# First three pairs: the causal mask added to the row-maximum blocks by TensorE instead of VectorE

## The chip, the cores and the metric

The kernel runs on one core of one Trainium2 chip. The metric is the device time of one execution in microseconds, the median of several runs.

## What is computed

The reference is a masked attention with a decay bias, whose output goes through a mixture of four attention experts, of which each row uses two. The part that the change touches is the subtraction of the row maximum under a causal mask:

```
scores = scale * q @ k.T                                   # 8 batches x 8 heads, 576 x 576, head_dim 64
bias   = -(cum[:, :, :, None] - cum[:, :, None, :])        # cum = running sum of max(s, 0)
scores = where(causal, -1e9, scores + minimum(bias, 0))
scores = scores - max(scores, axis=-1)
attn   = exp(scores); attn = attn / (sum(attn) + 1e-9); attn_out = attn @ v
# then per expert e: q, k, v = x @ wq[e], x @ wk[e], x @ wv[e]; the same masked softmax without bias;
# out += gate weight * (a @ v @ wo[e]) for the two best experts of each row
```

## The kernel before, in words

All work is cut into 50 steps called pairs: two heads of a batch (32 of them), two experts of a batch (16), or, twice near the end, projections alone. A pair's two heads are numbered j = 0 and 1. For each pair n the kernel splits q and k into a high and a low part (h and l steps, ScalarE, GpSimd and VectorE, L560 to L606), finds a maximum for every row, computes the transposed scores in PSUM chunks of 512 columns by two matmuls each (L687 and L692), takes the exponential on ScalarE (L708), clears the part above the diagonal on GpSimd (L726) and multiplies with v on TensorE (L844).

The row maxima come before the scores, because minus the maximum enters the scores as one more row of the second matmul (row 96 of Q2). They are found from bfloat16 products of q and k: the 576 rows are cut in nine blocks of 64, and block qt needs the columns 0 to 64 (qt + 1). The table MBANKS packs these blocks into six PSUM banks, called m0 to m5 as steps on TensorE and M0 to M5 as steps on VectorE; each entry has a slot, 0 to 8 for the blocks, and 9 for the left part of block 8, which is split in two.

- On TensorE (`bank`, L626) every slot is one matmul per head: 96 rows of contraction, 64 stationary columns, 64 to 512 moving columns. Head 0 writes PSUM partitions 0 to 63, head 1 partitions 64 to 127. LDWEIGHTS is an instruction of its own here.
- On VectorE (`reduce`, L640) every slot is one fused instruction that adds the mask (0, or -1e30 above the diagonal, in the last 64 columns of the block) and takes the maximum, followed by a second instruction that reads the accumulator into a column of `mcol`. The entry of slot 8 starts from the value of slot 9.
- When all nine columns are there, `mt` (TensorE, L660) transposes them, `mA` (ScalarE, L664) copies them with a minus sign, and `mq` (SyncE, L669) sends them by DMA into row 96 of Q2. The second matmul of every score chunk (L692) reads that row.

The order of all steps on all engines is one written list, STEPS; each engine executes its own instructions in that order, and PSUM banks are handed out in it (`take`, `give`), so that a bank given back by VectorE or ScalarE goes to a later step of TensorE. The maxima of pair n are computed during pairs n-2 and n-1. In the first 54 us the list also holds dummy matmuls (`idle`, L1325): 32 ahead of everything and 48 strewn between the steps (`z0` to `z47`); they write to a bank that nobody reads. The profile shows each as two records of 0.11 us.

`ident` (an identity in fp32) and `mask` (bfloat16) are made by GpSimd at the start.

Of the kernel before, what the change touches and what calls it, by code (L numbers as in the profile page):

```python
# [10 lines left out]
BF16 = mybir.dt.bfloat16  # L11
I32 = mybir.dt.int32
AF = mybir.ActivationFunctionType
OP = mybir.AluOpType
AX = mybir.AxisListType
# [3 lines left out]
S = 576  # L19
# [8 lines left out]

EARLY = 9
SUMMED = 4  # L30
FIRST_IDLE, IDLE = 32, 48
SCHUNKS = [
# [18 lines left out]
def chunks(n):  # L51
    return EARLY_SCHUNKS if n < EARLY else SCHUNKS
# [28 lines left out]
def heads(t, at, c0, c1):  # L81
# [5 lines left out]
MBANKS = [  # L87
# [6 lines left out]
]  # L94
# [239 lines left out]
def tile_attention_then_moe(ctx, tc, qk, vm, vt, s, wqk, wvg, wo, out):  # L334
    nc = tc.nc
# [25 lines left out]
    ident = PB[0][:, PSPARE : PSPARE + P]  # L361
# [5 lines left out]
    mask = const.tile([P, S], BF16, tag="mask", name="mask")  # L367
# [92 lines left out]
    def take(name):  # L460
        t = ps.tile([P, 512], F32, tag=f"bank{banks[0]}", name=name, bufs=1)
        taken[id(t)] = t, banks.pop(0)
        return t

    def give(t):
        banks.append(taken.pop(id(t))[1])
# [17 lines left out]
    mcol = {}  # L484
# [11 lines left out]
    def live(n):  # L496
        return 0 <= n < N and pairs[n][0] > 0
# [32 lines left out]
    def r2(n):  # L530
        return n % NQK2
# [82 lines left out]
    def maxima(n, banks):  # L614

        if not live(n):
            return {}
        items = {}

        def bank(bi):  # L620
            mbank[n, bi] = t = take(f"mx{n}_{bi}")
            for qt, k0, k1, c0, _ in MBANKS[bi]:
                for j in range(2):
                    q2 = Q2[r2(n)][:, j].bitcast(BF16)[:, 1::2]
                    k2 = K2[r2(n)][:, j].bitcast(BF16)[:, 1::2]
                    nc.tensor.matmul(  # L626
                        t[64 * j : 64 * j + 64, c0 : c0 + k1 - k0],
                        q2[0:RC, 64 * qt : 64 * qt + 64],
                        k2[0:RC, k0:k1],
                        start=True, stop=True,  # L630
                    )

        def reduce(bi):
            if n not in mcol:
                mcol[n] = sb.tile([P, 10], F32, tag="mcol", name=f"mcol{n}", bufs=2)
            t = mbank[n, bi]
            for qt, k0, k1, c0, slot in MBANKS[bi]:
                w = k1 - k0
                m0 = k0 + S - 64 * (qt + 1)
                nc.vector.tensor_tensor_reduce(  # L640
                    t[:, c0 : c0 + w], t[:, c0 : c0 + w], mask[:, m0 : m0 + w],
                    scale=1.0, scalar=mcol[n][:, 9:10] if slot == 8 else NEG, op0=OP.add, op1=OP.max,
                    accum_out=mcol[n][:, slot : slot + 1],
                )
            give(t)

        for bi in banks:
            items[f"m{bi}"] = lambda bi=bi: bank(bi)
            items[f"M{bi}"] = lambda bi=bi: reduce(bi)
        return items  # L650
# [24 lines left out]
    def scores(n):  # L675
# [49 lines left out]
        def lower(a, w):  # L725
            nc.gpsimd.affine_select(  # L726
                out=a, in_=a, pattern=[[0, a.shape[1]], [1, w]], compare_op=OP.is_ge,
                fill=0.0, base=0, channel_multiplier=-1,
            )

        def two_diags(ci):
            base = pchunk(n)[ci][0][0]
            lower(p[:, base : base + 1280].rearrange("p (b c) -> p b c", c=320)[:, :, 0:128], 128)

        def chunk_of(ci, c0, c1):
            at, o = pchunk(n)[ci]
            return heads(p, at, o + c0, o + c1)

        def sums_of():
            if n not in rtile:  # L740
                rtile[n] = sb.tile([P, 2, S], F32, tag="r", name=f"r{n}", bufs=3)
            return rtile[n]

        def first():
            r, a = sums_of()[:, :, 0:128], chunk_of(0, 0, 128)
            if n < SUMMED:
                nc.gpsimd.tensor_scalar(r, a, 1.0, 0.0, op0=OP.mult, op1=OP.add)
# [3 lines left out]
        def below(ci):  # L751
            if ci < 2 or n >= SUMMED:
                r = sums_of()
            if ci == 0 and n < EARLY:
                two_diags(0)
                add(r[:, :, 128:320], chunk_of(0, 128, 320), chunk_of(0, 320, 512), op=OP.add)
            elif ci == 0:
                lower(chunk_of(0, 224, 352), 128)
                nc.gpsimd.tensor_scalar(
                    r[:, :, 0:128], chunk_of(0, 224, 352), 1.0, 0.0, op0=OP.mult, op1=OP.add  # L760
                )
                lower(chunk_of(0, 0, 128), 128)
                add(r[:, :, 128:288], chunk_of(0, 352, 512), chunk_of(0, 0, 160), op=OP.add)
            elif ci == 1 and n < EARLY:
                add(r[:, :, 320:S], chunk_of(1, 0, 256), chunk_of(1, 256, 512), op=OP.add)
            elif ci == 1:
                add(r[:, :, 288:352], chunk_of(1, 0, 64), chunk_of(0, 160, 224), op=OP.add)  # L767
                add(r[:, :, 352:S], chunk_of(1, 64, 288), chunk_of(1, 288, 512), op=OP.add)
            elif ci == 2:
                two_diags(2)  # L770
                if n >= SUMMED:
                    for kt, q0, _, c in chunks(n)[2]:
                        add(r[:, :, q0:S], r[:, :, q0:S], chunk_of(2, c, c + S - q0), op=OP.add)  # L773
            else:
                a = heads(p, PTAIL, 0, 64)
                lower(a[0:64], 64)
                if n >= SUMMED:
                    nc.gpsimd.tensor_tensor(r[:, :, 512:S], r[:, :, 512:S], a, op=OP.add)
# [38 lines left out]
        if n < EARLY:  # L817
            items["e0"] = first
        if n < SUMMED:
            items["b0"] = early_sums  # L820
# [62 lines left out]
    def sums(n):  # L883

        if n not in quads or n < SUMMED:
            return {}
# [455 lines left out]
    def slot(n):  # L1342
# [11 lines left out]
        if n == N - 1:  # L1354
            steps.update(finish(n - 1, "x"))
            steps.update(finish(n, "y"))
            steps.update({{"v": "w", "V": "W"}[x[0]] + x[1:]: f for x, f in pv(n).items()})
            steps.update(numbered(proj_o(B - 2, range(4))))
            steps.update(out_here(B - 1))
        else:  # L1360
            steps.update(maxima(n + 1, (3, 4, 5)))
            steps.update(maxima(n + 2, (0, 1, 2)))
            steps.update(minus_max(n + 1))
            steps.update(hi(n + 2))
            steps.update(lo(n + 1))
            steps.update(sums(n - 1))
            steps.update(recip(n - 2))
            if n > -2:
                for x, f in enumerate(load(n + 3)):
                    steps["ld"] = f  # L1370
            for f in load_v(n):
                steps["lv"] = f
            for x, w in enumerate(WS.get(n, [])):
                steps[f"w{x}"] = w
# [62 lines left out]
```

## Time and profile before

| what | us |
|---|---|
| median of 3 runs (645.58, 645.64, 651.75) | 645.64 |
| the profiled execution | 645.95 |
| its span, first to last instruction | 644.2 |
| busy: TensorE matmul, weight load | 635.4 (99%), 543.0 (84%) |
| busy: VectorE, ScalarE, GpSimd | 546.1 (85%), 449.2 (70%), 433.3 (67%) |
| L640 fused maximum, 432 + 48 instructions; its accumulator reads | 194.2 (432 of them), 65.3 (480) |

The span is 1.7 us shorter than the execution, which also holds what lies before the first and behind the last instruction. A matmul's busy time covers its way through the array, and matmuls overlap: a 64-column one is shown with 0.19 to 0.22 us, while the next starts 0.06 us later. So the time that TensorE needs for one is read from the starts of neighbours, and a busy share of 99% leaves room for waits that are no longer than such an overlap.

### The profile page before, as it was taken

To read this page: it belongs to the slowest core of one execution; us is meant where nothing else is said; L and a number is where in the kernel's file an instruction comes from. 1 tells how busy PE (TensorE), PEld (TensorE's weight loads), DVE (VectorE), ACT (ScalarE), POOL (GpSimd) and SP (SyncE) were. 2 spreads that over 40 slices of the span, in tenths; PEclk is the share of its full clock that TensorE was granted. 3 is DMA by queue.
4 is the path that set the end of the run, shared out by engine and by line. 5 is a ranking of instruction groups with operands and counts; after the bars stand their busy time and mean duration, and the time that the engine had idled before them with its cause. 6 is when DMAs were issued, how large, how long until landed. Compare 5 with 4: busy or idle time off the path is not lost.

```text
span 644.2 us, 16548 instructions
## 1 busy us (share of the span) xinstructions
PE 635.4 (99%) x5990; PEld 543.0 (84%) x5990; DVE 546.1 (85%) x1440; ACT 449.2 (70%) x981; POOL 433.3 (67%) x530
## 2 busy tenths in 40 slices
PE   9999999999999999999999999999999999999997
PEld 9878898778878888888888898888987889789875
DVE  8988989898898978987898878898788978873984
ACT  6688767865877577766777766975685966566374
POOL 8786679686675868558766758559686777818030
PEclk9999999999999999999999999999999999999999
DMA  5356445436565375443756447475465634332323
GB/s 166 114 147 173 134 114 136 126 81 150 133 159 153 96 201 131 95 137 75 185 147 194 122 125 145 132 179 131 106 136 149 166 93 126 105 83 66 83 67 114
DMA packets 60879, 83.33 MB, mean 129 GB/s; under 512 B 26894, under 2 KB 35342, under 8 KB 60798
## 3 DMA queue, kind: packets, MB, share of 16 engines
q1 hardware_dynamic: 60798, 82.28, 49.0%
q8 instruction: 47, 0.77, 0.5%
q14 instruction: 34, 0.28, 0.2%
HBM read 44.55 MB, written 10.09 MB: 85 GB/s over the span
## 4 chain that ended last, share of the span: by engine, by line
PE 87%; DVE 6%; DMA 3%; issue 1%; ACT 1%; POOL 1%; SPq 0%; DVEq 0%; POOLq 0%
PE pvp L844 18%; PE pq L1078 16%; PE s L687 11%; PE s L692 10%; PE mx L626 9%; PE pw L1078 7%; PE po L1078 7%; PE sm L894 3%; DVE mx L640 3%; PE idle L1325 2%; DMA w_qk<-in_wqk_dram 2%; DMA rb<-rr 2%; PE po L1048 1%; PE mt L660 1%; PE gt L1205 1%
## 5 line engine op out<-in xcount | busy, mean ns | idle before, releaser
L640 DVE CUSTOM_DVE_ANT_0 mx<-mx,mask 128x256 f32<-128x256 f32 (+7 forms) x432 | 194.2, 468 | 33.2 <-PE mx L626 19.5
L708 ACT ACTIVATE p<-s 128x512 f32<-128x512 f32 x288 | 161.5, 588 | 60.9 <-PE s L692 57.7
L726 POOL TENSOR_SCALAR_AFFINE_SELECT p<-p 128x256 f32<-128x256 f32 (+2 forms) x183 | 112.7, 617 | 102.7 <-ACT p L708 96.1
L687 PE MATMUL s<-q,k 128*128 128x288 f32 (+5 forms) x672 | 168.9, 285 | 1.9 <-DVE mcol L640 0.8
L692 PE MATMUL s<-q,k 97*128 97x288 f32 (+5 forms) x672 | 160.9, 280 | 0.1
L687 PEld LDWEIGHTS s<-q,k 128*128 128x128 f32 (+1 forms) x672 | 122.5, 182 | 10.9 <-issue 4.7
L773 POOL TENSOR_TENSOR r<-r,p 128x640 f32<-128x640 f32 x84 | 120.8, 1438 | 6.8
L692 PEld LDWEIGHTS s<-q,k 97*128 97x128 f32 (+1 forms) x672 | 121.7, 182 | 1.3 <-DMA q<-mr 0.3
L600 DVE TENSOR_TENSOR q<-raw,q 64x576 fp32r<-64x576 f32 (+1 forms) x86 | 84.8, 995 | 19.1 <-ACT q L560 14.2
L844 PE MATMUL pvp<-p,v 128*64 128x320 f32 (+6 forms) x1024 | 96.3, 334 | 0.3 <-DVE mcol L640 0.3
L844 PEld LDWEIGHTS pvp<-p,v 128*64 128x64 f32 x1024 | 67.4, 137 | 25.5 <-issue 0.9
L605 DVE TENSOR_TENSOR k<-raw,k 64x576 fp32r<-64x576 f32 (+1 forms) x86 | 84.2, 986 | 5.5 <-DMA k<-k 3.5
L626 PE MATMUL mx<-k,q 96*64 96x256 bf16 (+7 forms) x960 | 81.2, 293 | 0.1
L1078 PE MATMUL pq<-xh,wqkh 128*128 128x288 f32 x256 | 76.3, 298 | 0.0
L1078 PE MATMUL pq<-xl,wqkh 128*128 128x288 f32 x256 | 75.5, 295 | 0.6 <-DVE xl L969 0.6
L1078 PE MATMUL pq<-xh,wqkl 128*128 128x288 f32 x256 | 75.4, 295 | 0.0
L626 PEld LDWEIGHTS <-q 96*64 96x64 bf16 x960 | 48.7, 109 | 20.7 <-issue 7.0
L563 ACT ACTIVATE k<-raw 64x576 fp32r<-64x576 f32 x96 | 64.6, 680 | 2.3 <-DMA raw<-in_qk_dram 0.6
L640 DVE DVE_READ_ACCUMULATOR2_ANT mcol<- 128x1 f32 x480 | 65.3, 136 | 0.9
L560 ACT ACTIVATE q<-raw 64x576 fp32r<-64x576 f32 x96 | 64.1, 679 | 1.9 <-DVE mcol L640 0.4
L858 ACT ACTIVATE pv<-pvp 128x320 f32<-128x320 f32 (+1 forms) x92 | 35.8, 402 | 33.1 <-PE pvp L844 32.8
L767 POOL TENSOR_TENSOR r<-p 128x128 f32<-128x128 f32 x37 | 21.5, 581 | 49.6 <-ACT p L708 49.5
(155 smaller groups left out, 1219.5 us busy)
## 6 DMA issues: line engine op xcount, KB each, us to landing
raw<-in_qk_dram SPq DMA_DIRECT2D x30, 576.0 KB
rb<-rr SPq DMA_DIRECT2D x92, 144.0 KB
q<-q SPq DMA_DIRECT2D x45, 288.0 KB
k<-k SPq DMA_DIRECT2D x39, 288.0 KB
v<-in_vm_dram SPq DMA_DIRECT2D x32, 256.0 KB
out_dram<-o SPq DMA_DIRECT2D x31, 256.0 KB
q<-mr SPq DMA_DIRECT2D x96, 2.2 KB
out_dram<-o SPq DMA_DIRECT2D x10, 128.0 KB
```

Source lines behind the costliest of these rows:

```text
L563: nc.scalar.activation(k2[0:64, j], get_raw(n, j)[64:128], AF.Copy)
L600: eng.tensor_tensor(a[64:128, j], get_raw(n, j)[0:64], q2[0:64, j].bitcast(F32), op=OP.subtract)
L605: eng.tensor_tensor(c[0:64, j], get_raw(n, j)[64:128], c[64:128, j].bitcast(F32), op=OP.subtract)
L626: nc.tensor.matmul(t[64 * j : 64 * j + 64, c0 : c0 + k1 - k0], q2[0:RC, 64 * qt : 64 * qt + 64], k2[0:RC, k0:k1], start=True, stop=True,)
L640: nc.vector.tensor_tensor_reduce(t[:, c0 : c0 + w], t[:, c0 : c0 + w], mask[:, m0 : m0 + w], scale=1.0, scalar=mcol[n][:, 9:10] if slot == ...
L687: nc.tensor.matmul(t[0:nk, c0 : c0 + q1 - q0], K1[r1(n)][:, j, k0 : k0 + nk], Q1[r1(n)][:, j, q0:q1], start=True, stop=False,)
L692: nc.tensor.matmul(t[0:nk, c0 : c0 + q1 - q0], K2[r2(n)][0 : RM + 1, j, k0 : k0 + nk], Q2[r2(n)][0 : RM + 1, j, q0:q1], start=False, stop= ...
L708: nc.scalar.activation(chunk_of(ci, 0, 512)[:, x % 2], tl[x], AF.Exp, scale=0.125)
L726: nc.gpsimd.affine_select(out=a, in_=a, pattern=[[0, a.shape[1]], [1, w]], compare_op=OP.is_ge, fill=0.0, base=0, channel_multiplier=-1,)
L773: add(r[:, :, q0:S], r[:, :, q0:S], chunk_of(2, c, c + S - q0), op=OP.add)
L844: nc.tensor.matmul(cur[h][64 * j : 64 * j + 64, q0 - PVC[h] : q1 - PVC[h]], vsl(j, kt), heads(ptile[n], at, c, c + q1 - q0)[:, j], start=f ...
L1078: nc.tensor.matmul(t[0:nk, 0:w], l, r, start=(x == 0), stop=(x == len(terms) - 1))
```

## The change

For pairs 0, 1 and 2 (`PLAIN = 3`), TensorE adds the mask itself: after the two products of a slot below 8 come two more matmuls, one per head, that accumulate into the last 64 columns of the block. Their stationary operand is the identity (read as the upper halves of its fp32 numbers), their moving operand the 64 x 64 triangle of `mask`. VectorE then takes a plain maximum of every slot except 8, written straight into `mcol`. Slot 9 has no diagonal and needs no mask; slot 8 keeps the fused instruction. STEPS and the number of dummies stay.

```
+PLAIN = 3
 ...
         def bank(bi):
             mbank[n, bi] = t = take(f"mx{n}_{bi}")
-            for qt, k0, k1, c0, _ in MBANKS[bi]:
+            for qt, k0, k1, c0, slot in MBANKS[bi]:
                 for j in range(2):
 ...
-                        start=True, stop=True,
+                        start=True, stop=not (n < PLAIN and slot < 8),
                     )
+                if n < PLAIN and slot < 8:
+                    for j in range(2):
+                        nc.tensor.matmul(
+                            t[64 * j : 64 * j + 64, c0 + k1 - k0 - 64 : c0 + k1 - k0],
+                            ident.bitcast(BF16)[0:64, 1:128:2], mask[0:64, S - 64 : S],
+                            start=False, stop=True,
+                        )
 ...
             for qt, k0, k1, c0, slot in MBANKS[bi]:
                 w = k1 - k0
                 m0 = k0 + S - 64 * (qt + 1)
+                if n < PLAIN and slot != 8:
+                    nc.vector.tensor_reduce(
+                        mcol[n][:, slot : slot + 1], t[:, c0 : c0 + w], axis=AX.X, op=OP.max
+                    )
+                    continue
                 nc.vector.tensor_tensor_reduce(
```

In the program the new matmuls use 64 rows and 64 columns of the array; the products of L626 use 96 rows, for which the program sets a tile of 128 rows by 64 columns. In the changed kernel's numbering L626 is L627, the new matmuls are L635, the plain maxima L649, the fused ones L653, and the dummies L1338.

TensorE, the start of bank m0 of pair 0 (q_0, k_0 are Q2 and K2 of pair 0, mx_0 the bank), before:

```order
L626 LDWEIGHTS q_0_68
L626 MATMUL mx_0_190<-k_0_71,q_0_68 64x448
L626 LDWEIGHTS q_0_68
L626 MATMUL mx_0_190<-k_0_71,q_0_68 64x448
L626 LDWEIGHTS q_0_68
L626 MATMUL mx_0_190<-k_0_71,q_0_68 64x64
```

and in the changed kernel (p_74 holds the identity):

```order
L627 LDWEIGHTS q_0_68
L627 MATMUL mx_0_190<-k_0_71,q_0_68 64x448
L635 LDWEIGHTS p_74
L635 MATMUL mx_0_190<-mask,p_74 64x64
L635 LDWEIGHTS p_74
L635 MATMUL mx_0_190<-mask,p_74 64x64
L627 LDWEIGHTS q_0_68
L627 MATMUL mx_0_190<-k_0_71,q_0_68 64x64
L627 LDWEIGHTS q_0_68
L627 MATMUL mx_0_190<-k_0_71,q_0_68 64x64
L635 LDWEIGHTS p_74
L635 MATMUL mx_0_190<-mask,p_74 64x64
```

Between the products of slot 6 and those of slot 0, and behind the latter, stand two masks each; the same holds for all eight slots of a pair.

TensorE, around the transposition mt of pair 0, ahead of which bank m0 of pair 1 ends; before:

```order
L626 LDWEIGHTS q_1_69
L626 MATMUL mx_0_268<-k_1_72,q_1_69 64x64
L1325 MATMUL idle<-p_75 64x128
L660 MATMUL mt_274<-p_74,mcol_200 9x128
L626 LDWEIGHTS q_1_69
L626 MATMUL mx_5_276<-k_1_72,q_1_69 64x256
```

and in the changed kernel:

```order
L627 LDWEIGHTS q_1_69
L627 MATMUL mx_0_290<-k_1_72,q_1_69 64x64
L635 LDWEIGHTS p_74
L635 MATMUL mx_0_290<-mask,p_74 64x64
L635 LDWEIGHTS p_74
L635 MATMUL mx_0_290<-mask,p_74 64x64
L1338 MATMUL idle<-p_75 64x128
L673 MATMUL mt_300<-p_74,mcol_208 9x128
L627 LDWEIGHTS q_1_69
L627 MATMUL mx_5_302<-k_1_72,q_1_69 64x256
```

The masks of 13 slots (eight of pair 0, five of pair 1) now stand ahead of mt; the number and place of the dummies is the same.

VectorE, the maxima of pair 0 (ISA is the fused instruction, and the row without an input its accumulator read), before, and the same place in the changed kernel:

```order
L640 ISA mx_0_190,mcol_200<-mx_0_190,mask 128x448
L640 ISA mcol_200 128x1
L640 ISA mx_0_190,mcol_200<-mx_0_190,mask 128x64
L640 ISA mcol_200 128x1
L640 ISA mx_1_195,mcol_200<-mx_1_195,mask 128x384
```

```order
L649 TENSOR_REDUCE mcol_208<-mx_0_190 128x1 x2
L649 TENSOR_REDUCE mcol_208<-mx_1_199 128x1 x2
L649 TENSOR_REDUCE mcol_208<-mx_3_230 128x1
L649 TENSOR_REDUCE mcol_208<-mx_2_211 128x1 x2
L649 TENSOR_REDUCE mcol_208<-mx_5_223 128x1 x2
L653 ISA mx_4_235,mcol_208<-mx_4_235,mask,mcol_208 128x320
```

Nine of a pair's ten fused instructions and their reads become nine single instructions; the banks come in the same order.

## Rows read from the trace of the kernel before

**Rows 1.** The page's chain that ended last, as shares of the span by engine and line.

```profile
PE pvp L844 18%; PE pq L1078 16%; PE s L687 11%; PE s L692 10%; PE mx L626 9%; PE pw L1078 7%; PE po L1078 7%; PE sm L894 3%; DVE mx L640 3%; PE idle L1325 2%; DMA w_qk<-in_wqk_dram 2%; DMA rb<-rr 2%; PE po L1048 1%; PE mt L660 1%; PE gt L1205 1%
```

**Rows 2.** Busy time by stretches: stretch, its us, then busy us (and instructions) of PE, PEld, DVE, ACT and POOL, the granted TensorE clock, the DMA share and GB/s.

```profile
12.00:20.10 8.10, 7.79 (x89) 6.70 (x87) 7.25 (x29) 3.68 (x7) 7.85 (x6) 1.00 0.40 96
...
41.00:72.00 31.00, 29.80 (x329) 24.59 (x326) 26.94 (x71) 24.18 (x49) 22.70 (x22) 1.00 0.55 143
72.00:110.00 38.00, 38.00 (x362) 34.12 (x361) 34.37 (x81) 27.43 (x61) 28.69 (x26) 1.00 0.49 131
```

**Rows 3.** The same chain in order of time: start, us, what.

```profile
12.80 0.63 DVE mx L640
...
71.44 0.39 PE s L687
```

**Rows 4.** TensorE in order of time from 12.2 us: start, us, engine, line, operation, out and in, rows*columns of the array, operand, count; in brackets the idle time before and what ended it. The maxima of pair 0 (x19), dummies, those of pair 1 (x9), a dummy, mt of pair 0.

```profile
12.24 1.45 PE L626 MATMUL mx<-k,q 96*64 96x64 bf16 x19
13.53 3.05 PE L1325 MATMUL idle<-p 128*64 128x128 f32 x26
...
16.57 0.92 PE L626 MATMUL mx<-k,q 96*64 96x320 bf16 x9
17.32 0.41 PE L1325 MATMUL idle<-p 128*64 128x128 f32 x2
18.04 0.28 PE L660 MATMUL mt<-p,mcol 128*9 128x128 f32 x1 [0.31 <-DVE mcol L640]
```

**Rows 5.** The weight load of the first second-half matmul of pair 0's scores, in the same form.

```profile
20.54 0.19 PEld L692 LDWEIGHTS s<-q,k 97*128 97x128 f32 x1 [0.25 <-DMA q<-mr]
```

**Rows 6.** TensorE around the last four banks of pair 2's maxima, in the same form: the last score matmul of pair 0 (192 columns), the maxima, dummies, the first score matmul of pair 1.

```profile
23.90 0.28 PE L692 MATMUL s<-q,k 97*128 97x192 f32 x1
24.11 1.02 PE L626 MATMUL mx<-k,q 96*64 96x256 bf16 x12
24.96 0.61 PE L1325 MATMUL idle<-p 128*64 128x128 f32 x4
25.49 0.42 PE L687 MATMUL s<-q,k 128*128 128x320 f32 x1
```

**Rows 7.** TensorE's waits from 28 to 72 us, in the same form, each from the timeline of its surroundings.

```profile
32.48 0.92 PE L844 MATMUL pvp<-p,v 128*64 128x320 f32 x6 [0.29 <-DVE mcol L640]
...
38.17 0.38 PE L687 MATMUL s<-q,k 128*128 128x320 f32 x1 [0.19 <-DVE mcol L640]
...
47.72 0.39 PE L687 MATMUL s<-q,k 128*128 128x320 f32 x1 [0.49 <-DMA q<-q]
...
71.44 0.39 PE L687 MATMUL s<-q,k 128*128 128x320 f32 x1 [0.62 <-DVE mcol L640]
```

**Rows 8.** VectorE in order of time, in the same form: the first fused maximum of pair 1, the first of pair 2, and what follows the last of pair 2.

```profile
17.85 0.53 DVE L640 CUSTOM_DVE_ANT_0 mx<-mx,mask 128x320 f32<-128x320 f32 x1
...
22.77 0.60 DVE L640 CUSTOM_DVE_ANT_0 mx<-mx,mask 128x384 f32<-128x384 f32 x1
...
27.99 3.38 DVE L600 TENSOR_TENSOR q<-raw,q 64x1152 fp32r<-64x1152 f32 x1
```

**Rows 9.** VectorE's groups by shape over the whole span, costliest first but for the accumulator read: line, engine, operation, out and in, count, then busy us, mean ns of one, and idle time before.

```profile
L640 DVE CUSTOM_DVE_ANT_0 mx<-mx,mask 128x512 f32<-128x512 f32 x48 | 34.4, 716 | 4.2 <-PE mx L626 3.7 <-ACT rs L903 0.4
...
L640 DVE CUSTOM_DVE_ANT_0 mx<-mx,mask 128x64 f32<-128x64 f32 x48 | 11.2, 232 | 1.6
...
L640 DVE DVE_READ_ACCUMULATOR2_ANT mcol<- 128x1 f32 x480 | 65.3, 136 | 0.9
...
L1168 DVE TENSOR_REDUCE rk<-g 128x20 f32<-128x80 f32 x8 | 1.9, 236 | 0.3
...
L1187 DVE TENSOR_REDUCE gs<-ew 128x5 f32<-128x20 f32 x8 | 1.4, 175 | 0.3
```

**Rows 10.** TensorE around the one operation of this kernel that uses 64 rows of the array (L1205, a transposition of 64 x 4 numbers), at two places, ahead of them the same line with 128 rows, in the timeline's form.

```profile
201.22 0.28 PE L692 MATMUL s<-q,k 97*128 97x192 f32 x1
201.34 0.60 PE L1205 MATMUL gt<-p,p 128*4 128x128 f32 x4
...
349.37 0.22 PE L687 MATMUL s<-q,k 128*64 128x64 f32 x1
349.43 0.22 PE L692 MATMUL s<-q,k 97*64 97x64 f32 x1
349.58 0.21 PE L1205 MATMUL gt<-p,p 64*4 64x64 f32 x1
349.73 0.40 PE L687 MATMUL s<-q,k 128*128 128x288 f32 x1
349.96 0.29 PE L692 MATMUL s<-q,k 97*128 97x288 f32 x1
350.10 0.27 PE L687 MATMUL s<-q,k 128*128 128x224 f32 x1
...
505.31 0.21 PE L1205 MATMUL gt<-p,p 64*4 64x64 f32 x1
505.45 0.42 PE L626 MATMUL mx<-k,q 96*64 96x448 bf16 x4
505.71 0.41 PE L844 MATMUL pvp<-p,vx 128*64 128x256 f32 x2
```

**Rows 11.** GpSimd early in the program, in the same form: the end of making the mask.

```profile
2.92 0.53 POOL L371 TENSOR_SCALAR_AFFINE_SELECT mask<-mask 64x64 bf16<-64x64 bf16 x2
```

## The prediction

> **What bounds the kernel now.** I first read the chain that ended last: 87 of 100 parts of it are TensorE, so that TensorE is the bound over most of the span; VectorE's masked maxima (L640) are 3% and the dummies (L1325) 2% [rows 1]. In order of time, these 3% lie at the start: the chain runs through VectorE's maxima from 12.80 us on, and from 71.44 us on through TensorE [rows 3]. The stretches say the same: from 72 to 110 us TensorE is busy for 38.00 of 38.00 us, whereas before 72 us it waits now and then; the granted clock is 1.00, the 2.4 GHz level, in all of them [rows 2]. Whatever moves the moment at which TensorE gets to its work of 72 us moves the end by as much. So the question is what TensorE itself does up to there, and its waits there are few: 0.31 us for the last maximum of pair 0 [rows 4], 0.25 for the DMA of minus the maximum [rows 5], and 0.29, 0.19, 0.49 and 0.62 later [rows 7]. In between it executes what STEPS gives it, dummies included, one behind the other: VectorE looks like the chain at 12 to 28 us, but TensorE is about as late. That is the thing to see here: a chain through VectorE doesn't mean that TensorE has room.
>
> A wait is longer than shown by the part of the matmul ahead that overlaps a successor: a dummy is shown with 0.27 us and followed after 0.11, so 0.16 more. I count 0.47 for mt, 0.25 for the DMA, 0.45 and 0.35 for the next two, 0.65 and 0.78 for the last two.
>
> **VectorE's side.** Nine of ten maxima in each of three pairs lose the accumulator read, 27 in all. Pair 1 takes from 17.85 to 22.77, 4.92 us, for 2880 columns [rows 8]. The shapes give (716 - 232) / 448 = 1.08 ns per column [rows 9], so 3.11 us are columns and 1.81 / 10 = 0.18 us the fixed part of a fused maximum with its read. No plain maximum out of PSUM is in this trace. The nearest rows take 236 ns for 80 columns and 175 for 20 [rows 9]: 1.02 ns per column and 0.155 fixed, without overlap of a successor. So a plain one saves between 0.03 us and, if the whole read's 0.136 [rows 9] goes, 0.14: 0.7 to 3.7 us in all, all of it before the L600 at 27.99 [rows 8]. A loss isn't excluded by a row, but nothing speaks for one, since both kinds read PSUM column by column. I take 0.1 each, 2.7 us, between the ends.
>
> **TensorE's side.** Each of the 8 slots below 8 in three pairs, 24 in all, gets two masks of 64 columns.
> - Streaming: the last four banks of pair 2 are six products per head, 1856 columns, from 24.11 to 24.96 [rows 6]: 0.46 ns per column with both heads side by side, so 0.03 us for a pair of masks.
> - Changing the shape: the masks use 64 rows of the array, the products around them 96. The trace has one operation with 64 rows, the L1205 transposition. It starts 0.15 us behind a 64-column matmul, where such a one is otherwise followed after 0.06 (349.37, 349.43, 349.58), and its successor starts 0.15 us behind it: 0.09 on either side. The same line with 128 rows follows a 192-column matmul after 0.12 (201.22, 201.34), without a gap. So the rows make the gap [rows 10]. When it goes over to maxima (505.45 to 505.71), 512 columns take 0.26 us, where 0.235 are expected: another 0.03 for the first weights. I take 0.03 + 0.09 + 0.09 + 0.03 = 0.24 us for a slot.
> - Bounds: 0.03, if bfloat16 masks pay no change; and, if weights can't be loaded ahead across a change, 0.03 + 4 x 0.09 = 0.39, since the first score matmul behind a change is followed after 0.23 us, not 0.14 (349.73, 349.96, 350.10) [rows 10]. Below nothing it can't be, for 48 matmuls come on top. I take 0.24, nearest to the rows with the same neighbours.
>
> The Trainium skill, TensorEngine Tiling (Array Packing), Key Properties, speaks against this change: going over to another tiling mode, not just another tile, drains the engine. By that rule every slot pays twice, bfloat16 or not, as in my sum, and the first rival below would fall away; the trace agrees for the fp32 transposition (0.09 us), and the page has no price. The same page, Instruction Overhead, gives every matmul about 60 cycles however few its columns: 25 ns at 2.4 GHz (estimate), so 0.05 us for two masks if they go one behind the other, and 0.5 us more in all; the trace's pairs go side by side, and the sum goes by them.
>
> **The sum,** in TensorE's order, against the execution profiled (645.95, of which 644.2 are the span).
> 1. 13 slots stand ahead of mt of pair 0: 13 x 0.24 = 3.1 us. The wait of 0.47 goes, as VectorE is done earlier than that: bank m3 of pair 0 is complete by about 13.53 - 0.15 (m4 behind it) + 8 x 0.24 = 15.3 [rows 4], and the 1856 columns and seven operations left take 2.3 to 3.3 us, to 18.6 at the latest, while TensorE comes to mt at 20.7. So mt moves by 2.65. The masks wait for nothing themselves: the triangle is done at 3.45 us [rows 11].
> 2. Seven more slots before pair 0's scores: 1.7. The last of them precedes a change that was there anyway: -0.1. The DMA that follows mt has moved by 2.65 alone, so its 0.25 go: 4.0.
> 3. Four more slots (m5, m0 and m3 of pair 2): 1.0, so pair 1's scores, at 25.49 before, start 5.0 us later.
> 4. VectorE's gain is lost here: it waits for products. Pair 2's m3 is complete at 24.96 + 5.0 = 30.0; two banks later, at 31.3, comes the L600 that started at 27.99, and the maxima of pair 3 behind it are 3.9 us late. TensorE, 5.0 late, finds them done, and its waits of 0.45 and 0.35 go: 4.2.
> 5. ScalarE, GpSimd, SyncE's queue and the weight and row loads behind it follow from steps that have moved as much, so most of the last two waits (1.43) stays. I take off a third, 0.4, since VectorE is a little less late than TensorE.
>
> That leaves 3.8 us at 72 us, and from there TensorE has no wait to take it up. The execution profiled is 0.3 above the median of 645.64; on the median the forecast is 645.64 + 3.8 = 649.4. With 0.22 to 0.28 us for a slot, and none or two thirds of the last waits gone, it is 2.7 to 5.1 more: 648.3 to 650.7.
>
> **Rivals.**
> - The masks pay no change (0.03 us a slot). Then TensorE has 0.7 us more in all, its waits of 0.47, 0.25, 0.45 and 0.35 go against it since VectorE is 1 us ahead per pair: 0.7 - 1.5 = -0.8, so 644.8, not slower. For it: all else around the masks is bfloat16 with 64 columns, and separate weight loads; against it: rows 10. It decides below 0.06 us a slot (24 x 0.06 = 1.5).
> - The change is paid, but all waits up to 72 us go, the 1.43 too: 24 x 0.22 - 0.1 - 2.95 = +2.2, so 647.9. For it: the last two waits are for a DMA and for VectorE, not for TensorE [rows 7]; against it: both lie behind steps that move.
> - Weights are exposed at each change (0.39): 9.4 - 0.1 - 1.5 - 0.4 = +7.4, so 653.0, slower by over 1%. For it: the scores behind the 64-row transposition; against it: the maxima behind it pay 0.03.
>
> **How the numbers follow.** Forecast 0.62, no change paid 0.14, all waits gone 0.13, exposed weights 0.11. Over 1% is 6.5 us, about what a measurement of this kernel tells from no change. VectorE can't give that back (3.7 at most): faster 0.01. Slower is the third rival: 0.11; the rest, 0.88, is within 1%. The range runs from just under the first rival, 644.6, to 652.4, short of the third; the forecast's own is 648.3 to 650.7.
>
> **What would show it.** Right: 48 records of the mask product, with 0.2 to 0.27 us more per slot between neighbouring products; mt of pair 0 at about 20.7 with no wait; VectorE idle for some 3 us between 13 and 31 us with TensorE's maxima as what ended it; the first score matmul of pair 1 at 30.5, and the work of 72.0 at 75.8. Wrong: products in front of and behind the masks that follow without a gap (first rival), TensorE's waits at 47 and 71 us gone (second), slots over 0.35 us (third), a granted clock below 1.00 at 12 to 30 us, or a plain maximum that is slower than the fused one with its read by so much that mt still waits.

## The result, and the profile after

The changed kernel takes 654.38 us (median of 19 runs, 651.73 to 656.23), the kernel before beside it 646.88 (19 runs, 645.07 to 653.70). The ratio is 1.0095, with a 95% interval of 1.0074 to 1.0117: slower by about 1%, 6.1 us of 646.88. It is taken from undisturbed executions alone, so it need not be that of the medians. The forecast was 649.4, that is 3.8 us more than the kernel before, with a range up to 652.4: the sign was right, the size was not.

The execution profiled took 653.39 us, with a span of 651.7 against 644.2, so it has 7.5 us to explain. The stretches first, as in [rows 2]:

```profile
12.00:20.10 8.10, 8.10 (x66) 6.49 (x64) 4.35 (x12) 3.35 (x6) 7.85 (x6) 0.79 0.39 96
...
41.00:72.00 31.00, 29.13 (x329) 24.75 (x331) 28.22 (x67) 24.26 (x51) 19.63 (x21) 1.00 0.58 166
72.00:110.00 38.00, 38.00 (x362) 34.12 (x361) 33.99 (x78) 28.04 (x61) 29.34 (x26) 1.00 0.43 116
```

The number behind the five engines' busy times, the granted clock, is the one to see: from 12 to 20.1 us the granted clock is 0.79, where before it was 1.00. A mean of 0.79 between the levels of 1.0 (2.4 GHz) and 0.5 (1.2 GHz) is (1 - 0.79) x 8.10 / 0.5 = 3.4 us at the lower one. TensorE in order of time over pair 0's maxima, answering to [rows 4] (starts and durations in us):

```profile
11.91 0.42 PE L627 MATMUL mx<-k,q 96*64 96x448 bf16 x2
12.26 0.22 PE L635 MATMUL mx<-mask,p 64*64 64x64 bf16 x2
12.41 0.22 PE L627 MATMUL mx<-k,q 96*64 96x64 bf16 x2
12.56 0.22 PE L635 MATMUL mx<-mask,p 64*64 64x64 bf16 x2
...
15.24 0.44 PE L627 MATMUL mx<-k,q 96*64 96x320 bf16 x2
15.47 4.62 PE L1338 MATMUL idle<-p 128*64 128x128 f32 x26
```

Two things stand here. A 64-column pair of products at 12.41 is followed by its masks after 0.15 us, and masks are followed by the next product after 0.15 (12.26 to 12.41); without masks 64 columns would be worth 0.03. So a slot pays 0.15 + 0.15 - 0.03 = 0.27 us. And the 26 dummies behind the group take 4.62 us, the same 26 before 3.05 [rows 4]: here lies the stretch of the lower clock, and it costs 1.57 us.

TensorE's waits up to 80 us, answering to [rows 4, 5, 7]: mt of pair 0, then the score matmuls.

```profile
22.16 0.43 PE L1338 MATMUL idle<-p 128*64 128x128 f32 x2
22.52 0.28 PE L673 MATMUL mt<-p,mcol 128*9 128x128 f32 x1
...
43.09 0.36 PE L700 MATMUL s<-q,k 128*128 128x256 f32 x1 [0.87 <-DVE k L606]
45.55 0.39 PE L700 MATMUL s<-q,k 128*128 128x320 f32 x1 [0.21 <-DVE mcol L653]
55.32 0.39 PE L700 MATMUL s<-q,k 128*128 128x320 f32 x1 [0.70 <-DMA q<-q]
...
78.26 0.34 PE L700 MATMUL s<-q,k 128*128 128x320 f32 x1
```

mt waits no more, nor does the matmul of 32.48, nor the last of them (71.44 before). The waits at 38.17 and 47.72 are still there (0.21 and 0.70), and one of 0.87 us is new, at the first score matmul of pair 2, for VectorE's k step (L606; L605 before). VectorE over the same time, answering to [rows 8]:

```profile
21.50 2.02 DVE L649 TENSOR_REDUCE mcol<-mx 128x1 f32<-128x320 f32 x5 [3.34 <-PE mx L635]
...
30.75 0.76 DVE L649 TENSOR_REDUCE mcol<-mx 128x1 f32<-128x256 f32 x2 [2.85 <-PE mx L627]
...
33.52 3.75 DVE L601 TENSOR_TENSOR q<-raw,q 64x1152 fp32r<-64x1152 f32 x1
...
40.17 0.69 DVE L450 TENSOR_TENSOR wqkl<-w_qk,wqkh 128x512 fp32r<-128x512 f32 x1 [0.67 <-ACT wqkh L449]
40.88 2.07 DVE L606 TENSOR_TENSOR k<-raw,k 64x1152 fp32r<-64x1152 f32 x1
```

What it gained it waits away for products, 3.34 and 2.85 us in these two places alone; its k step takes 2.07 us. The weight remainder ahead of the k step (L450; L449 before) waits for ScalarE's step that makes the upper half of the same weights. ScalarE in the kernel before, then ScalarE and GpSimd in the changed kernel:

```profile
32.50 0.63 ACT L448 ACTIVATE wqkh<-w_qk 128x512 fp32r<-128x512 f32 x1
...
39.51 0.63 ACT L449 ACTIVATE wqkh<-w_qk 128x512 fp32r<-128x512 f32 x1
40.27 1.46 POOL L769 TENSOR_TENSOR r<-p 128x384 f32<-128x384 f32 x1
```

So ScalarE's step is 7.01 us later than before, and the k step starts 7.01 later too (40.88 against 33.87), with GpSimd's L769 under way.

To place the loss I follow one instruction, the score matmul that stood at 71.44 us. It starts at 78.26, 6.82 later, so nine tenths of the span's 7.5 us are lost by then; in the stretch behind it TensorE is busy for 38.00 of 38.00 us, as before.

### The profile page after: what moved, and what is told of

The parts are those of the page before. It is cut to its first block, busy times and chain, and to the rows that moved or that the text cites. A ratio compares the mean times of both kernels' runs of the same rounds, so it can differ in the third digit from the quotient of the medians.

```text
span 651.7 us, 16616 instructions
## 1 busy us (share of the span) xinstructions
PE 642.6 (99%) x6038; PEld 546.9 (84%) x6038; DVE 547.8 (84%) x1413; ACT 448.9 (69%) x981; POOL 433.0 (66%) x530
## 4 chain that ended last, share of the span: by engine, by line
PE 89%; DVE 3%; ACT 3%; DMA 2%; SPq 1%; issue 1%; ACTq 0%; DVEq 0%
PE pvp L857 18%; PE pq L1091 15%; PE s L700 11%; PE s L705 10%; PE mx L627 9%; PE pw L1091 7%; PE po L1091 6%; PE sm L907 3%; PE idle L1338 3%; DVE mx L653 1%; PE po L1061 1%; SPq L949 1%; PE mt L673 1%; ACT p L721 1%; PE pw L1146 1%
## 5 line engine op out<-in xcount | busy, mean ns | idle before, releaser
L653 DVE CUSTOM_DVE_ANT_0 mx<-mx,mask 128x192 f32<-128x192 f32 (+7 forms) x405 | 182.3, 468 | 33.4 <-PE mx L627 18.0
L739 POOL TENSOR_SCALAR_AFFINE_SELECT p<-p 128x256 f32<-128x256 f32 (+2 forms) x183 | 114.7, 628 | 111.9 <-ACT p L721 100.5
L606 DVE TENSOR_TENSOR k<-raw,k 64x576 fp32r<-64x576 f32 (+1 forms) x86 | 85.1, 997 | 3.3 <-DMA k<-k 1.2
L627 PE MATMUL mx<-k,q 96*64 96x256 bf16 (+7 forms) x960 | 85.2, 294 | 0.1
L627 PEld LDWEIGHTS <-q 96*64 96x64 bf16 x960 | 48.6, 109 | 21.1 <-issue 6.6
L653 DVE DVE_READ_ACCUMULATOR2_ANT mcol<- 128x1 f32 x453 | 61.7, 136 | 0.8
```

The lines of the kernel that those rows point to most:

```text
L606: eng.tensor_tensor(c[0:64, j], get_raw(n, j)[64:128], c[64:128, j].bitcast(F32), op=OP.subtract)
L627: nc.tensor.matmul(t[64 * j : 64 * j + 64, c0 : c0 + k1 - k0], q2[0:RC, 64 * qt : 64 * qt + 64], k2[0:RC, k0:k1], start=True, stop=not (n ...
L653: nc.vector.tensor_tensor_reduce(t[:, c0 : c0 + w], t[:, c0 : c0 + w], mask[:, m0 : m0 + w], scale=1.0, scalar=mcol[n][:, 9:10] if slot == ...
L739: nc.gpsimd.affine_select(out=a, in_=a, pattern=[[0, a.shape[1]], [1, w]], compare_op=OP.is_ge, fill=0.0, base=0, channel_multiplier=-1,)
```

## The experiments

For all of them this matmul's start against 71.44 ("lag at 71") is given beside the ratio to the kernel before. It rests on one execution each. Two executions of the kernel before differ in it by 0.08 us, two of the changed kernel by 0.66, since the wait at 47.72 came in one of them alone. So differences below some 0.7 us say nothing here; where less is at stake I take the lag of the score matmul of 38.17, ahead of that wait, which is +7.39 and +7.45 in the two traces of the changed kernel.

**b1_before: the kernel before, a second trace; a1_after: the changed kernel, a second trace.** No edit.

> The kernel before once more, for a second trace. Theory (which of VectorE and GpSimd starts first at about 33 us is set by the program and is turned round by the change): again VectorE's weight remainder (L449) at 33.2 us ahead of GpSimd's clear, VectorE's k step (L605) in 1.7 us, and no wait of TensorE for it. Rival (chance of the run): the k step takes 2.0 us or more here and TensorE waits 0.9 us for it.

> The changed kernel once more, for a second trace and more times. Theory (the fall of the granted clock belongs to pair 0's masked group, though not to every execution): either the clock falls again between 14 and 20 us and TensorE stands 6.5 to 7.5 us behind before at 72 us, or it does not and TensorE stands 5 to 5.5 us behind. Either way a wait of 0.9 us for VectorE's k step. 5.5 to 7.5 us above before in the times.

The second trace of before has the k step in 1.69 us again, no wait for it, and a lag at 71 of +0.08. So what follows is no chance of one run up to there. Behind 250 us it is: this execution took 650.37 us, and 1.9 us of the difference are a wait for nothing that the profile shows, in one place:

```profile
273.31 0.34 PE L687 MATMUL s<-q,k 128*128 128x224 f32 x1 [1.85 <-issue]
```

So differences late in a single trace mean little here, and I use those up to 80 us. The changed kernel has in its second trace (654.89 us, ratio 1.0106, 1.0047 to 1.0165) the mean clock of 0.79 from 12 to 20.1 us again and a k step of 2.07; the lag at 71 is +6.16, a little under the 6.5 to 7.5 expected with a fall of the clock, because the wait at 47.72 is gone here too. The dummies:

```profile
15.47 4.68 PE L1338 MATMUL idle<-p 128*64 128x128 f32 x26
```

**e1_rows96: no change of shape.**

```
-    ident.bitcast(BF16)[0:64, 1:128:2], mask[0:64, S - 64 : S],
+    ident.bitcast(BF16)[0:RC, 1:128:2], mask[0:RC, S - 64 : S],
```

> The 48 masks with 96 rows of the array instead of 64 (identity and triangle taken with their zero rows below), so that no product around them differs in shape; all else as in the changed kernel. Theory (the change of shape drains TensorE on both sides, 0.09 us each, and the drained group of pair 0 is followed by a fall of the granted clock): a slot costs 0.03 to 0.06 us instead of 0.24, the granted clock stays at 1.00 from 12 to 30 us, VectorE's plain maxima now take waits away from TensorE, and the time is within 1 us of the kernel before (645 to 647 where that is 646), 5 to 7 us under the changed kernel. Rival A (mask products cost as such: 48 more matmuls and weight loads, not the change of shape): slots stay near 0.2 us and the time stays 4 to 6 us above before. Rival B (the plain maxima and what stands behind them on VectorE cost the time): TensorE waits for VectorE at pair 2's scores as in the changed kernel, and at least 1 us of the loss stays.

Measured: 648.01 us (12 runs), before 647.14, ratio 0.9997 (0.9970 to 1.0025); lag at 71 +1.31. The whole loss of the changed kernel that the times show goes when 48 matmuls become larger. At pair 1's first score matmul (25.49 before) the lag is +0.52 with 0.72 of waits gone, so a slot costs some 0.05 us (estimate). TensorE at pair 0's maxima, at the dummies behind them and at the first score matmul of pair 2:

```profile
12.83 0.36 PE L627 MATMUL mx<-k,q 96*64 96x384 bf16 x2
12.88 0.20 PE L635 MATMUL mx<-mask,p 96*64 96x64 bf16 x1
12.92 0.34 PE L627 MATMUL mx<-k,q 96*64 96x384 bf16 x1
13.03 0.19 PE L635 MATMUL mx<-mask,p 96*64 96x64 bf16 x1
...
14.17 3.05 PE L1338 MATMUL idle<-p 128*64 128x128 f32 x26
...
37.04 0.36 PE L700 MATMUL s<-q,k 128*128 128x256 f32 x1 [0.96 <-DVE k L606]
```

The masks slip in beside the other head's products, with no gap; the dummies are at full clock. Rival A, that the masks cost as such, falls. But the wait for the k step stays, 0.96 us, which was rival B's mark; the 1 us of loss that it named too is in this trace's lag, not in the times.

**e2_masks_only: TensorE's side alone.**

```
-    if n < PLAIN and slot != 8:
+    if False and slot != 8:
```

> TensorE's masks as in the changed kernel, VectorE keeps the fused maximum (which adds the mask a second time). Theory: VectorE's gain is lost in waiting for products anyway, so the time is that of the changed kernel within 1.5 us, about 5 to 8 us above before, with the fall of the granted clock behind pair 0's maxima. Rival B (the plain maxima cost the time): 2 us or more under the changed kernel.

Measured: 653.84 us (7 runs), ratio 1.0100 (1.0067 to 1.0133), lag at 71 +6.03. VectorE's plain maxima are worth nothing once TensorE has the gaps around the masks, and they are not what makes TensorE wait for the k step either: here, where every maximum is fused, it waits 0.9 us. That is the end of rival B as it was put; the wait itself remains to be explained. In this trace the clock did not fall although TensorE's instructions are those of the changed kernel. The dummies, a product that comes up again below, and the wait:

```profile
15.31 3.05 PE L1338 MATMUL idle<-p 128*64 128x128 f32 x26
...
38.66 0.31 PE L627 MATMUL mx<-k,q 96*64 96x320 bf16 x1
...
41.36 0.36 PE L700 MATMUL s<-q,k 128*128 128x256 f32 x1 [0.87 <-DVE k L606]
```

Without the fall the lag at 38.17 is +5.66, 1.7 us under the changed kernel's; at 71 only 0.8 of this is left, as the waits at 47.72 (0.88) and 71.44 (0.59) are both there in this trace. Of its seven runs five have a mean granted clock of 0.997 or less (653.38 to 655.92 us), two have 0.999 and 1.000 (651.63, the trace, and 651.50). A mean over a whole execution doesn't say where the clock fell, so these runs show a fall somewhere in five of seven, not that it comes behind pair 0.

**e3_plain_only: VectorE's side alone**, without mask products, so that the diagonal blocks of three pairs stay unmasked.

```
-    if n < PLAIN and slot < 8:            # TensorE
+    if False and slot < 8:
```

> VectorE's plain maxima alone, no mask products: the diagonal blocks of pairs 0 to 2 are left unmasked in the maxima. Theory: TensorE's waits of 0.47, 0.25, 0.45 and 0.35 us before 40 us go, some 1 to 1.5 us, and the time is 0.5 to 1.5 us under before, granted clock 1.00. Rival B: at or above before, with a wait of TensorE for VectorE's k step of pair 2.

Measured: 646.87 us (10 runs), ratio 1.0013 (0.9980 to 1.0046), lag at 71 -0.37. A miss: I expected 0.5 to 1.5 us of gain. The gain on VectorE is real, 17.20 to 21.05 us for pair 1's maxima, 3.85 us instead of 4.92 [rows 8], 0.12 for each plain one. By 33 us TensorE is 0.5 us ahead, and then loses 1.0 to the same wait for the k step:

```profile
36.16 0.36 PE L700 MATMUL s<-q,k 128*128 128x256 f32 x1 [0.96 <-DVE k L606]
```

That is what rival B had said of this run. So without any masks VectorE's gain buys nothing that the times show; the interval leaves room for 1.3 us.

**e4_grouped: masks behind all products of a bank**, 15 changes of shape there and back instead of 24.

```
-                        start=True, stop=not (n < PLAIN and slot < 8),
+                        start=n >= PLAIN or c0 == 0, stop=n >= PLAIN or slot == 8,
                     )
+            for qt, k0, k1, c0, slot in MBANKS[bi]:
                 if n < PLAIN and slot < 8:
 ...
-                            start=False, stop=True,
+                            start=False, stop=slot == MBANKS[bi][-1][4] or slot in (3,),
```

> The masks of a bank behind all its products: five changes of shape and back per pair instead of eight, 15 instead of 24, with the same 48 masks of 64 rows. Theory (the change costs, not the mask): 9 x 0.2 = 1.8 us less than the changed kernel, 4 to 5 us above before; the fall of the clock is shorter or stays. Rival A (each mask costs): the time of the changed kernel.

Measured: 651.18 us (10 runs), ratio 1.0054 (1.0026 to 1.0081), lag at 71 +2.99; that is 3.5 us above before, where 4 to 5 were expected. The 48 masks are the same. Against e2_masks_only, whose early clock was 1.00 as well, the lag at 71 is 3.0 us smaller, of which 0.8 are the wait at 71.44 that only e2_masks_only has. Ahead of the waits, the TensorE product that stood at 33.92 us before starts at 36.56 instead of 38.66:

```profile
36.56 0.31 PE L627 MATMUL mx<-k,q 96*64 96x320 bf16 x1
```

That is 2.1 us for 9 changes, 0.23 each. The change costs, not the mask. The mean clock of this trace is 0.996 all the same: it fell for 3.4 us between 138 and 142 us, among score matmuls and projections, where no mask stands.

**e5_order: e1_rows96, and GpSimd a little later.**

```
 def late_constants():
-    nc.gpsimd.memset(vx[64:128, 4], 0.0)
+    for _ in range(3):
+        nc.gpsimd.memset(vx[64:128, 4], 0.0)
```

> Masks with 96 rows as in e1_rows96, and GpSimd makes one of its late constants three times instead of once, so that its clear behind them starts some 0.5 us later, behind VectorE's weight remainder. Theory (the two engines shut each other out and the one that starts first goes on): VectorE's remainder takes 0.7 us instead of 1.13 and its k step 1.7 instead of 2.07, TensorE's wait of 1.0 us for it goes, GpSimd is late instead and nobody waits for that; the time is 0.5 to 1.5 us under that of e1_rows96, at or slightly under before. Rival: the k step stays at 2 us and the time with e1_rows96.

Measured: 646.56 us (12 runs), before 648.25, ratio 0.9974 (0.9945 to 1.0003), lag at 71 -0.25, 1.56 under that of e1_rows96. The two engines at about 33 us, in the kernel before (VectorE, then GpSimd):

```profile
33.16 0.69 DVE L449 TENSOR_TENSOR wqkl<-w_qk,wqkh 128x512 fp32r<-128x512 f32 x1
33.87 1.69 DVE L605 TENSOR_TENSOR k<-raw,k 64x1152 fp32r<-64x1152 f32 x1
...
33.29 1.06 POOL L726 TENSOR_SCALAR_AFFINE_SELECT p<-p 128x512 f32<-128x512 f32 x1
34.43 1.99 POOL L756 TENSOR_TENSOR r<-p 128x384 f32<-128x384 f32 x1
```

in e1_rows96:

```profile
33.68 1.13 DVE L450 TENSOR_TENSOR wqkl<-w_qk,wqkh 128x512 fp32r<-128x512 f32 x1
34.82 2.07 DVE L606 TENSOR_TENSOR k<-raw,k 64x1152 fp32r<-64x1152 f32 x1
...
33.63 0.63 POOL L739 TENSOR_SCALAR_AFFINE_SELECT p<-p 128x512 f32<-128x512 f32 x1
34.35 1.33 POOL L769 TENSOR_TENSOR r<-p 128x384 f32<-128x384 f32 x1
```

and in e5_order:

```profile
33.60 0.69 DVE L451 TENSOR_TENSOR wqkl<-w_qk,wqkh 128x512 fp32r<-128x512 f32 x1
34.30 1.35 DVE L607 TENSOR_TENSOR k<-raw,k 64x1152 fp32r<-64x1152 f32 x1
...
34.30 1.85 POOL L740 TENSOR_SCALAR_AFFINE_SELECT p<-p 128x512 f32<-128x512 f32 x1
```

Whichever starts first runs at its own pace, and the other is stretched: before, VectorE came 0.13 us ahead of GpSimd's clear, which took 1.06 us, and the k step, starting with the clear under way, 1.69; in e1_rows96 it came 0.05 us behind, and paid, with 1.13 for the remainder and 2.07 for the k step; with GpSimd held back it has 0.69 and 1.35, and the clear takes 1.85. The Trainium skill, SBUF — State Buffer, Who interferes with whom, says that a VectorE instruction with two inputs in SBUF and a GpSimd instruction that reads SBUF keep each other out, and that the order of issue decides who waits; these rows agree. So 0.2 us of earlier or later arrival turned into nearly 1 us on TensorE in e1_rows96. Of the kernels here that leave nothing out this is the fastest, but its interval still holds no change at all, and overlaps that of e1_rows96.

**a2_order: the same on the changed kernel**, with `range(8)` in place of `range(3)` and masks of 64 rows.

> The changed kernel, masks with 64 rows, and GpSimd makes one of its late constants eight times instead of once, so that its clear comes some 1.7 us later, behind VectorE's remainder and about with its k step. Theory: the k step takes 1.35 to 1.7 us instead of 2.07 and TensorE's wait of 0.9 us for it shrinks to 0.6 or less or goes; TensorE stands 0.4 to 0.9 us nearer to the kernel before at 45 us than in the changed kernel; drains and the fall of the clock stay, 5 to 7 us above before. Rival: the wait stays at 0.9 us.

Measured: 653.98 us (8 runs), ratio 1.0071 (1.0035 to 1.0107). The k step takes 1.35 us and TensorE's wait for it is gone, as expected; but a little ahead of it TensorE now waits 0.43 us for a GpSimd constant behind the added ones. From pair 1's first score matmul to that of 38.17 the lag falls by 0.24 us, where it grows by 0.38 in the changed kernel: 0.6 us better. The lag at 71, +8.58, does not show it, since the clock stayed low for longer, 6.8 us from 14.6 us on:

```profile
16.40 5.47 PE L1339 MATMUL idle<-p 128*64 128x128 f32 x26
...
42.70 0.34 PE L858 MATMUL pvp<-p,v 128*64 128x64 f32 x4 [0.43 <-POOL v L403]
```

The times are 4.6 us above before, where 5 to 7 were expected. The ratio lies 0.24 to 0.35% under those of the changed kernel, but the intervals overlap; that it shortens the whole is not shown.

**e6_late: the change in pairs 12 to 14.**

```
-    if n < PLAIN and slot < 8:
+    if 12 <= n < 15 and slot < 8:
```

> The change made in pairs 12 to 14 instead of 0 to 2, where TensorE has hardly any waits and no dummies stand between its steps. Theory: 24 slots at 0.24 us and nothing gained on VectorE, 5.0 to 6.5 us above before, without a fall of the granted clock. Rival (much of the loss belongs to the start: the clock, the turned order at 33 us): under 4.5 us.

Measured: 652.47 us (10 runs), before 648.25, ratio 1.0064 (1.0034 to 1.0094): 4.1 us, under the 4.5 of the rival, though the interval (2.2 to 6.1) reaches into the theory's 5.0 to 6.5. The trace is clearer. Pair 13's maxima, from the first product to the step behind them, before:

```profile
153.75 1.48 PE L626 MATMUL mx<-k,q 96*64 96x448 bf16 x20
155.06 0.44 PE L844 MATMUL pvp<-p,v 128*64 128x320 f32 x2
```

and here:

```profile
154.99 0.39 PE L627 MATMUL mx<-k,q 96*64 96x448 bf16 x2
155.31 0.22 PE L635 MATMUL mx<-mask,p 64*64 64x64 bf16 x2
...
158.28 0.22 PE L635 MATMUL mx<-mask,p 64*64 64x64 bf16 x2
158.43 0.49 PE L857 MATMUL pvp<-p,v 128*64 128x320 f32 x2
```

That is 3.44 us instead of 1.31, 0.27 for each of eight slots, as at the start; the clock stays at 1.00. 24 slots at that rate (2.13 for eight) are 6.4 us, and the lag of the score matmuls goes from -0.4 us ahead of the first mask (130.64 in the kernel before) to +5.6 behind the last (171.24): 6.0 us in the trace. The ratio gives less; why is not shown. The executions of the kernel before that it is taken against spread from 644.25 to 652.55 us.

**e7_pairs12: pair 0 left as before.**

```
-    if n < PLAIN and slot < 8:
+    if 0 < n < PLAIN and slot < 8:
```

> The change in pairs 1 and 2 alone; pair 0 as before. Theory (a slot costs 0.27 us; the fall of the granted clock belongs to pair 0's eight masked slots in a row): 16 slots at 0.27, 4.3 us, and no fall of the clock before 30 us; VectorE's k step is shut out as before, 0.9 us; TensorE stands 3.5 to 4.5 us behind the kernel before at 73 us, and the times are 2.5 to 4 us under the changed kernel. Rival (the fall comes from anything that shifts the start, or from the masks of pair 1): the clock falls all the same, and the times are at most 2 us under the changed kernel.

Measured: 651.77 us (10 runs), ratio 1.0052 (1.0024 to 1.0080), lag at 71 +3.20, 3.6 under the changed kernel (I had expected 3.5 to 4.5 of lag). The dummies:

```profile
13.35 3.05 PE L1338 MATMUL idle<-p 128*64 128x128 f32 x26
```

At 38.17 it stands at +3.68, 3.7 under the changed kernel. So eight slots of pair 0 are worth 8 x 0.27 = 2.2 us by themselves and some 1.5 through the clock. Before 30 us the clock falls in three of the four traces with pair 0's masks on 64 rows in every slot (not in that of e2_masks_only) and in none of the other eight. The clocks of the runs point the same way, as far as a mean over an execution can: with pair 0's masks on 64 rows in every slot (the changed kernel twice, e2_masks_only, a2_order) 32 of 38 runs have a mean granted clock of 0.997 or less, with them grouped (e4_grouped) 6 of 10, with pair 0 left alone or given 96 rows (e1_rows96, e3_plain_only, e5_order, e6_late, e7_pairs12) 14 of 54, and the kernel before, timed beside these, 21 of 72.

## Why the prediction was wrong

**Right: the price of a slot and its cause.** 0.24 us forecast from one fp32 transposition, 0.27 measured, bfloat16 or not. The shape is the cause: 96 rows instead of 64 take it away. The rule of the Trainium skill that the prediction weighed (TensorEngine Tiling (Array Packing), Key Properties: another mode drains, another tile doesn't) is borne out by e1_rows96. The first rival, masks that pay no change, is out. The third forecast 653.0, near what came, but for a reason that the traces don't bear out: with exposed weights a slot would have been 0.39, so its number was near by luck. The 0.03 missing on 24 slots are 0.7 us.

**Right: steps 1 to 3, as long as the clock holds.** In e2_masks_only, with the clock at 1.00, mt of pair 0 comes at 20.79 us without a wait (20.7 forecast), and pair 1's first score matmul is 5.28 us late (5.0 forecast). In the changed kernel it is 7.01 late.

**Right: VectorE's gain is lost** (step 4), and its size, 0.12 us for a maximum against 0.1.

**Wrong, the largest: the clock.** The prediction took 1.00 from [rows 2] for the kernel after as well, and named a lower one only as a sign of being wrong. It had no term and no rival for it. In both traces of the changed kernel 3.4 us at 1.2 GHz begin as pair 0's maxima end, which have a gap on either side of every mask, and cost 1.6 us; in the trace of a2_order it is 6.8 us, and 2.4 us on the dummies alone. That pair 0's masks bring the fall about rests on counting traces (three of four against none of eight); it is likely, not proven. That the dummies of the first 54 us fill TensorE's gaps was in front of me; a change that opens 16 new gaps among them should have raised the question. What exactly TensorE must do to keep the clock was not tried. The clock is not the whole either: the two executions of the changed kernel with a mean clock of 0.999 and 1.000 took 652.39 and 651.73 us, still above the forecast's own 650.7.

**Wrong: step 4's waits.** It took away both, 0.45 and 0.35, since VectorE's maxima of pair 3 would be less late than TensorE. The first did go, but between the two lies the k step, for which nobody waited before, and it now costs 0.87 us. The step compared the end of the maxima alone. The k step stands behind ScalarE's L449, which moved by the full 7.01 us, whereas TensorE, with the 0.54 of the first wait gone, had moved by 6.47; and it takes 2.07 us instead of 1.69. So of TensorE's 0.92 us (7.39 - 6.47) 0.54 are the gain paid back and 0.38 the longer k step. The step held that at its old duration, but it depends on what GpSimd does at the same time: a2_order and e5_order bring it down to 1.35.

**Near in one trace: step 5.** 0.4 off the last two waits was forecast; the one at 71.44 is gone (0.78) and the one at 47.72 grew by 0.2, 0.6 together. In the second trace both are gone, 1.3 together, which is the second rival's sign; so the third was a guess that happened to fit. (That rival's sum has 0.22 us a slot; with 0.24 it comes to +2.7, not +2.2.)

**The sum again**, to 71 us, in the profiled execution: 6.4 for the 24 slots (at 2.13 for eight, as in e6_late), 1.6 for the clock, 0.9 for the k step, less 0.47 and 0.25 at mt and the DMA, 0.1, 0.54 at 32.48 and 0.6 at the end: 6.9, and 6.82 was measured. The forecast had 3.8 there. Of the 3.0 between, 1.6 are the clock, 1.1 step 4's waits (0.9 paid and 0.3 kept, against 0.1 more of gain), 0.7 the slots, less 0.2 in step 5 and roundings. The terms don't simply add up from one execution to the next: the second trace has 6.16 with the same fall of the clock, and e2_masks_only 6.03 without it, because the waits at 47.72 and 71.44 come in some traces and not in others.

## What to carry to other kernels

Work handed to TensorE was priced here by whether it keeps the array's shape: the same mask on 96 rows with zeroes below cost some 0.05 us a slot, on 64 rows 0.27. Before taking the granted clock of the old trace for the new one, look for new gaps in the stretch where the old kernel spends dummies. And where VectorE and GpSimd contend, a shift can be worth some five times its length (0.18 us against nearly 1 in e1_rows96): check who starts first in each such pair, and whether the change turns it round. Follow every chain that an engine waits for, not the longest alone: the wait for the maxima went, and the k step behind ScalarE took its place.

## What the runs showed that was not expected

- The lower clock sets in as the gaps end (15.3 and 15.6 us in the two traces of the changed kernel) or among the last of them (14.6 in a2_order), and it is the work without gaps behind them that pays: 26 dummies in 4.62 and 4.68 us instead of 3.05.
- It is not in every execution of the same stream of TensorE's instructions: the trace of e2_masks_only has none. And it can come where no mask is: at 138 us in e4_grouped.
- A zero-padded product is cheaper than the smaller exact one: ratio 0.9997 against 1.0095, by two slice bounds.
- Holding GpSimd back by some 0.7 us (its clear starts at 34.30 instead of 33.63) moved TensorE forward by 1.2 us between 33.92 and 38.17 us of before (lag from 0.35 to 1.33 in e1_rows96, from 0.27 to 0.10 in e5_order).
